# Two more buffers for the natural rows of q and k, a ring of 2560 tokens for x, and 512-token blocks in slots 48 to 143

## The chip, the core and the metric

The kernel runs on one core of a Trainium2 chip. The metric is the device time of one execution in microseconds (us). The core has five engines that run side by side and meet at semaphores: TensorE (PE) for matmuls, VectorE (DVE), ScalarE (ACT), GpSimd (POOL) and SyncE (SP). GpSimd, SyncE and ScalarE also issue DMAs, which 16 DMA engines carry out.

## The reference

Attention in a sliding window, and a two-layer network behind it, cut to what matters:

```python
q, k, v: (8, 8, 576, 64)                     # batch, heads, tokens, head width
scores = q @ k.T / sqrt(64)                  # only where |i - j| <= 32
attn   = softmax(scores) @ v
x      = attn.transpose(0, 2, 1, 3).reshape(8 * 576, 512)
h      = x @ w_in                            # (4608, 512) @ (512, 2048)
g      = h if h >= 1, 0 if h <= -1, else (h + 1)**2 / 4
out    = g @ w_out                           # (4608, 2048) @ (2048, 512)
```

## The kernel before, in words

The matmuls run in bf16. The kernel is one stream of **slots**, numbered by `a` in the loop at L497, with an order written out by hand. A slot does three things on TensorE:

- **the projection** `hp`: a piece of x @ w_in. In a narrow slot (L528 to L532) that is 256 columns of w_in for one block of 256 tokens: 8 matmuls of 256 columns (L491). In a wide slot (L510 to L518, slots `WIDE`, 56 to 135) it is 128 columns of w_in for two blocks together: 4 matmuls of 512 columns (L516). Eight narrow slots do one block, 16 wide slots do two. ACT and DVE make g from `hp` (L535 to L542) and write it to `gT`, which holds four blocks of 256 tokens; `home` says in which of the four a block lies. `hp` has two buffers in PSUM.
- **attention** of some later tokens, if the table `ev` has any for this slot (`run(a)` behind the projection, `run(a + 0.5)` at the slot's end).
- **the output**: matmuls of g @ w_out of earlier blocks (`pair` at L466 in the early slots, `unit` at L451 after that; from slot 40 on 3 units in a slot, from slot 72 on 4). ACT copies the sums out, SP stores them.

**Attention** of a batch of 576 tokens has five steps. `scores` or `scores8` does q @ k on TensorE, exp on ACT, and the mask on DVE. `sums` does attn @ v and the row sums on TensorE; its `end()` makes 1/sum with a Ln (L303) and an Exp (L304) on ACT; the product that gives x is put off (`muls`) and issued on DVE by `flush` (L309, L312), at the latest at the start of the next slot. Steps 0 and 1 are tokens 0 to 223 for the lower and the upper half of a group of heads (y1 = 0 and 1), steps 2 and 3 are tokens 224 to 479, step 4 is the rest for both. The list `sl` gives the slots: entry n has the `sums` of step 6 + n and the `scores` of step 7 + n, counted from batch 1 on.

**x** lies in `xT`, 512 rows of x as four groups of 128 partitions, in a ring of `RING` = 2304 tokens. The projection's matmuls go over the four groups in the order 0, 2, 1, 3: the first half of them reads y1 = 0, the second y1 = 1.

**q and k** of batches 2 to 7 come in natural rows (`load_nat`, L95 to L100, GpSimd's queue, f32 to bf16 on the way, 64 elements to a row) and are transposed by a DMA from the SP queue (`xpose`, L196 to L199) into `qT` (three buffers) and `kT` (three buffers). The natural rows have one buffer each for two tags, `n0` and `n1`: q of batch b has tag (b % 2), k the other. So q of batch b + 1 goes where k of batch b lies, and can't be loaded until that is transposed. v has three buffers (`load_v`). All these loads stand in one order on GpSimd, each behind the one before; a transpose stands on SP behind the stores of the slots before it. The loop issues the loads and the transposes of batches 3 to 7 in slots counted from the first scores of that batch (L419 to L425): loads 17 slots ahead, transposes 11 and 9.

The pool `early` (L120) holds what is used up to slot 1 only: the first rows of q and k and a helper for the mask. It stays allocated to the end.

Of the kernel before, what the change touches and what calls it, by code (L numbers as in the profile page):

```python
# [8 lines left out]
BF = mybir.dt.bfloat16  # L9
# [5 lines left out]
def kernel(  # L15
# [19 lines left out]
    nc = tc.nc  # L35
    B, H, S, D = q.shape
# [3 lines left out]
    NU = NY * S // 128  # L40
    MAIN = 480
    TAIL = S - MAIN
    RING = 4 * S
    PAD = 32
    WIDE = 56, 136
    LONG = 2

    const = ctx.enter_context(tc.tile_pool(name="const", bufs=1))
    nat = ctx.enter_context(tc.tile_pool(name="nat", bufs=2))
# [19 lines left out]
    w_out = const.tile([128, 16, DM], BF, name="w_out")  # L69
    xT = const.tile([128, NY, RING], BF, name="xT")  # L70
    gT = const.tile([128, 16, 4, 256], BF, name="gT")
# [3 lines left out]
    V, P, A = nc.vector, nc.gpsimd, nc.scalar  # L75


    qn, kn, vn = {}, {}, {}
    HD = (slice(0, 64), slice(64, 128))

    def load_half(half, t, h, eng=None, x=None):
# [12 lines left out]

    def load_nat(b, t):  # L95
        src, dst, nm = ((q, qn, "qn"), (k, kn, "kn"))[t]
        x = dst[b] = nat.tile([128, NU, 2, D], BF, name=nm, tag=f"n{(b + t) % 2}", bufs=1)
        for h in range(2):
            nc.gpsimd.dma_start(out=x[:, :, h], in_=src[b, NY * h:NY * h + NY].rearrange("y s d -> (y s) d")  # L99
                                .rearrange("(u p) d -> p u d", p=128))  # L100
# [16 lines left out]
        nc.gpsimd.dma_start(out=w_out[:, k0:k1, 256 * c:256 * c + 256],  # L117
                            in_=moe_w_out.rearrange("(ko ki) f -> ki ko f", ki=128)[:, k0:k1, 256 * c:256 * c + 256])

    early = ctx.enter_context(tc.tile_pool(name="early", bufs=1))  # L120
    q32 = early.tile([128, 2, S], FP, name="q32")
    for h in range(2):
        load_half(0, 0, h, (nc.sync, nc.scalar)[h], q32)
# [145 lines left out]
    def sums(b, y1, lo, hi, pool=ps_n):  # L269

        bb = two_banks(pool)
        w = hi - lo
        todo = []
        if lo < MAIN:
            ys, D0 = (y1,), w
            for par in range(2):
                a0 = max(lo, 32 * par)
                off = 32 - 64 * par
                todo.append((None, a0 - lo, hi - lo, lambda a, h, par=par, a0=a0, off=off: (
                    pt[b][HD[a], h, y1, par, a0 + off:hi + off])))  # L280
                for c2 in range(4):
                    q0, q1 = max(0, 128 * c2 - off, lo), min(128 * c2 + 128 - off, hi)
                    if q0 < q1:
                        todo.append((NC * y1 + 2 * c2 + par, q0 - lo, q1 - lo, lambda a, h, par=par, q0=q0, q1=q1, off=off: (
                            pt[b][HD[a], h, y1, par, q0 + off:q1 + off])))
        else:
            ys, D0 = (0, 1), 2 * w
            todo.append((None, 0, 2 * w, lambda a, h: pt8[b][HD[a], h].rearrange("p y j -> p (y j)")))
            for y in ys:
                todo.append((NC * y + 8, y * w, y * w + w, lambda a, h, y=y: pt8[b][HD[a], h, y]))  # L290
                for c in (None, NC * y + 7):
                    todo.append((c, y * w, y * w + 64, lambda a, h, y=y: pt[b][HD[a], h, y, 1, 448:512]))
        for n, (c, c0, c1, p) in enumerate(todo):
            o = D0 if c is None else 0
            for a in range(2):
                for h in range(2):
                    nc.tensor.matmul(bb[HD[h], a, o + c0:o + c1], ones[HD[a]] if c is None else vn[b][HD[a], c, h],  # L297
                                     p(a, h), start=n == 0, stop=True, skip_group_check=True)

        def end():  # L300
            lr = smp.tile([128, 2, 256], FP, name="lr", bufs=1)
            rc = smp.tile([128, 2, 256], FP, name="rc")
            A.activation(lr[:, :, :D0], bb[:, :, D0:2 * D0], AF.Ln)  # L303
            A.activation(rc[:, :, :D0], lr[:, :, :D0], AF.Exp, scale=-1.0)  # L304
            r0 = (b * S + lo) % RING
            o = xT.rearrange("p (a y) t -> p a y t", a=2)[:, :, ys[0]:ys[-1] + 1, r0:r0 + w]
            if len(ys) == 1:
                o = o[:, :, 0]
                muls.append(lambda: V.tensor_mul(o, bb[:, :, :D0], rc[:, :, :D0]))  # L309
            else:  # L310
                like = "p a (y j) -> p a y j"
                muls.append(lambda: V.tensor_mul(o, bb[:, :, :D0].rearrange(like, y=2), rc[:, :, :D0].rearrange(like, y=2)))  # L312
        return end
# [96 lines left out]
        at(a, seq[2 + n][0])  # L410
    for n, a in enumerate((18, 20, 26.5, 28)):
        at(a, seq[3 + n][1])
    sl = [30, 32, 35, 38, 41, 44, 47, 50, 52, 57, 60, 63, 66, 68, 72, 76, 79, 82, 86]
    sl += [90, 93, 96, 100, 104, 108, 111, 114, 118, 123]
    for n, a in enumerate(sl):
        at(a, seq[6 + n][0], seq[7 + n][1] if n < len(sl) - 1 else None)
    for t in range(2):
        at(10 + 1.5 * t, (tposes, 1, (t, 0), (t, 1)))
    loads, xps = {}, {16: [(2, 0)], 18: [(2, 1)]}  # L419
    for b in range(LONG + 1, B):  # L420
        a = sl[5 * (b - 1) - 7] - 17
        for t in range(3):
            loads.setdefault(a + t, []).append((b, t))
        for t in range(2):
            xps.setdefault(a + 6 + 2 * t, []).append((b, t))  # L425

    op = {}

    def home(t):

        return (3 - t % 4 if t % 4 in (0, 3) else t % 4) if WIDE[0] <= NF * t < WIDE[1] else t % 4

    def unit(x):

        tt, j = divmod(x, 16)
        if tt == NT // 128 - 1:
            half, n = divmod(j, 8)
            if n == 0:
                op[tt] = ps_o.tile([128, 256], FP, name="op", tag="op")
            cols = slice(256 * half, 256 * half + 256)  # L440
            for k in (2 * n, 2 * n + 1):
                nc.tensor.matmul(op[tt], gT[:, k, home(tt // 2), 128 * (tt % 2):128 * (tt % 2) + 128], w_out[:, k, cols],  # L442
                                 start=k == 0, stop=k == 15)
            if n == 7:
                osb = osp.tile([128, 256], FP, name="osb")
                A.copy(osb, op[tt])
                nc.sync.dma_start(out=out[128 * tt:128 * tt + 128, cols], in_=osb)
            return
        if j == 0:
            op[tt] = ps_o.tile([128, DM], FP, name="op", tag="op")  # L450
        nc.tensor.matmul(op[tt], gT[:, j, home(tt // 2), 128 * (tt % 2):128 * (tt % 2) + 128], w_out[:, j],  # L451
                         start=j == 0, stop=j == 15)
        if j == 15:
            osb = osp.tile([128, DM], FP, name="osb")
            A.copy(osb, op[tt])  # L455
            nc.sync.dma_start(out=out[128 * tt:128 * tt + 128, :], in_=osb)
# [40 lines left out]
    for a in range(NF * NB + 2 * NF):  # L497
# [11 lines left out]
        if a < NF * NB:  # L509
            if wide:  # L510
                n, f = divmod(a - WIDE[0], 2 * NF)
                t = WIDE[0] // NF + 2 * n
                r0 = TB * t % RING
                hp = ps_h.tile([128, 2, TB], FP, name="hp", tag="hp")
                for n, kk in enumerate((0, 2, 1, 3)):
                    nc.tensor.matmul(hp.rearrange("p n t -> p (n t)"), w_in[:, kk, 128 * f:128 * f + 128],  # L516
                                     xT[:, kk, r0:r0 + 2 * TB], start=n == 0, stop=n == 3)
                g = gT[:, f, home(t):home(t + 1) + 1:home(t + 1) - home(t)]  # L518
            else:
                t, f = divmod(a, NF)  # L520
                r0 = TB * t % RING
                if a in (0,):
                    hps = [ps_h.tile([128, 2, TB], FP, name="hp", tag="hp") for _ in range(2)]
                    for y in range(2):
                        for n in range(2):
                            project(hps[n], f + n, r0, [(j, y + 2 * m) for j in range(2) for m in range(2)], y == 0, y == 1)
                elif not hps:
                    pool, tag = (ps_o, "op") if a == 6 else (ps_h, "hp")  # L528
                    hps = [pool.tile([128, 2, TB], FP, name="hp", tag=tag)]
                    project(hps[0], f, r0, [(j, kk) for j in range(2) for kk in (0, 2, 1, 3)], True, True)  # L530
                hp = hps.pop(0)
                g = gT[:, 2 * f:2 * f + 2, home(t)]  # L532

            rr = ewp.tile([128, 2, TB], FP, name="rr")
            A.activation(rr, hp, AF.Relu, scale=0.5, bias=0.5)  # L535
            mx = ewp.tile([128, 2, TB], FP, name="mx")
            if a in two_on_act:
                A.activation(mx, rr, AF.Square)
                V.scalar_tensor_tensor(g, hp, 1.0, mx, op0=ALU.max, op1=ALU.min)
            else:  # L540
                V.tensor_max(mx, hp, rr)  # L541
                V.scalar_tensor_tensor(g, rr, 1.0, mx, op0=ALU.min, op1=ALU.mult)  # L542
# [8 lines left out]
        if a >= 40:  # L551
# [2 lines left out]
                unit(x)  # L554
            done += n
        run(a + 0.5)
        for x in xps.get(a, []):
            xpose(*x)

# [29 lines left out]
```

## Time and profile before

| | us |
|---|---|
| median of 3 runs | 309.26 (307.13 to 311.13) |
| the profiled execution, its own time | 308.08 |
| its span in the profile | 306.3 |
| DVE busy / ACT busy / POOL busy | 241.8 / 190.6 / 78.2 |
| projection, narrow (L491): 512 matmuls | 66.2 busy |
| projection, wide (L516): 320 matmuls | 82.1 busy |
| output (L451): 496 matmuls | 126.9 busy |
| DMA queue of GpSimd's loads | 103,136 packets, 18.06 MB |
| DMA queue of stores and transposes | 34,016 packets, 16.81 MB |

The busy time of a group is the time in which at least one of its instructions ran. [...] A line of waits says which engine and instruction waited, for what, for how many us in total, how often and how long at most. In a line of the timeline stand the start, the duration, the engine, the line of the kernel and the tiles that are written and read; a bracket at its end is the idle time of that engine before it and what ended it. TensorE's granted clock is full (1.00) in every stretch.

### The profile page before, as it was taken

The page shows a single profiled execution, that of the slowest core. Times are in us where ns is not written, and L with a number is a line of the kernel's source. Part 1 is how long each engine was busy: PE and PEld are TensorE (multiplying, and loading weights), DVE is VectorE, ACT ScalarE, POOL GpSimd, SP SyncE. Part 2 cuts the span into 40 slices and gives each one's busy share as a digit, 9 for nine tenths or more (in the row PEclk, how much of TensorE's full clock was granted, in tenths as well). Part 3 has the DMA queues.
Part 4 walks back from the last instruction along what each step waited for, and adds up shares of the span by engine and source line. Part 5 has one row for each costly group of instructions (what it writes and reads, how often), then busy time and mean ns, then how long its engine had stood idle before and what let it go on. Part 6 is the DMA issues. An engine that isn't in the chain of part 4 may idle for free.

```text
span 306.3 us, 7848 instructions
## 1 busy us (share of the span) xinstructions
PE 298.4 (97%) x3324; PEld 175.0 (57%) x3324; DVE 241.8 (79%) x378; ACT 190.6 (62%) x318; POOL 78.2 (26%) x94
## 2 busy tenths in 40 slices
PE   8889999999999999999999999999999999999995
PEld 3567878876666776544444444444445444446644
DVE  4278958879888999999988888888888888788700
ACT  3687796648757767667766766665667654444311
POOL 8896661037008204601800730000000000000000
PEclk9999999999999999999999999999999999999999
DMA  9999999989999996997999997551011000000121
GB/s 153 184 195 201 178 185 179 165 152 159 127 155 145 151 142 122 171 155 121 147 154 177 108 170 77 113 112 36 34 36 37 34 36 35 34 36 34 58 81 68
DMA packets 137331, 35.67 MB, mean 116 GB/s; under 512 B 122320, under 2 KB 133072, under 8 KB 137296
## 3 DMA queue, kind: packets, MB, share of 16 engines
q0 software_dynamic: 103136, 18.06, 80.2%
q1 hardware_dynamic: 34016, 16.81, 26.8%
q8 instruction: 26, 0.43, 0.6%
q10 hardware_dynamic: 144, 0.29, 0.4%
q14 instruction: 9, 0.07, 0.1%
HBM read 36.70 MB, written 9.44 MB: 151 GB/s over the span
## 4 chain that ended last, share of the span: by engine, by line
PE 85%; DMA 8%; POOL 3%; ACT 1%; issue 1%; DVE 0%; POOLq 0%; ACTq 0%
PE op L451 34%; PE hp L516 23%; PE hp L491 14%; DMA kT<-kn 7%; PE bb L297 5%; PE op L466 5%; PE bb L231 2%; DMA w_in<-in_moe_w_in_dram 2%; POOL w_in L112 1%; PE op L442 1%; POOL vn L107 1%; PE tp L191 1%; POOL kh L86 1%; POOL qh L86 0%; PE bb L210 0%
## 5 line engine op out<-in xcount | busy, mean ns | idle before, releaser
L535 ACT ACTIVATE rr<-hp 128x512 f32<-128x512 f32 x144 | 85.5, 595 | 84.5 <-PE hp L516 49.5
L451 PE MATMUL op<-w_out,gT 128*128 128x512 bf16 x496 | 126.9, 380 | 0.0
L541 DVE TENSOR_TENSOR mx<-hp,rr 128x512 f32<-128x512 f32 x139 | 95.8, 689 | 26.7 <-ACT rr L535 24.9
L542 DVE SCALAR_TENSOR_TENSOR gT<-rr,mx 128x512 bf16<-128x512 f32 x139 | 96.4, 694 | 4.8
L516 PE MATMUL hp<-xT,w_in 128*128 128x512 bf16 x320 | 82.1, 379 | 0.0
L451 PEld LDWEIGHTS <-gT 128*128 128x128 bf16 x496 | 46.1, 98 | 47.6
L491 PE MATMUL hp<-xT,w_in 128*128 128x256 bf16 x512 | 66.2, 273 | 1.7 <-DMA w_in<-in_moe_w_in_dram 1.5
L491 PEld LDWEIGHTS <-w_in 128*128 128x128 bf16 x512 | 49.2, 98 | 17.0 <-DMA w_in<-in_moe_w_in_dram 1.3
L516 PEld LDWEIGHTS <-w_in 128*128 128x128 bf16 x320 | 31.3, 98 | 37.8
L99 POOL DMA_DIRECT2D qn<-in_q_dram x12 | 14.6, 1222 | 92.2 <-DMA kT<-kn 90.1
L239 ACT ACTIVATE pt<-bb 128x1024 bf16<-128x1024 f32 (+1 forms) x33 | 32.9, 1002 | 6.1 <-PE bb L231 4.7
L107 POOL DMA_DIRECT2D vn<-in_v_dram x32 | 27.5, 893 | 5.1 <-DMA w_out<-in_moe_w_out_dram 2.9
L309 DVE TENSOR_TENSOR xT<-bb,rc 128x512 bf16<-128x512 f32 (+1 forms) x32 | 21.0, 657 | 9.8 <-ACT rc L304 8.9
L455 ACT COPY osb<-op 128x512 f32<-128x512 f32 x31 | 18.0, 581 | 12.4 <-PE op L451 12.1
L304 ACT ACTIVATE rc<-lr 128x512 f32<-128x512 f32 (+2 forms) x40 | 23.5, 587 | 1.3
L303 ACT ACTIVATE lr<-bb 128x512 f32<-128x512 f32 (+2 forms) x40 | 22.0, 550 | 0.2
L205 DVE TENSOR_TENSOR pt<-pt,mask 128x1024 bf16<-128x1024 bf16 (+1 forms) x33 | 20.3, 615 | 0.8 <-ACT pt L239 0.7
L297 PE MATMUL bb<-pt,ones 64*64 64x256 bf16 (+3 forms) x352 | 19.5, 255 | 0.2 <-DVE xT L309 0.2
L297 PE MATMUL bb<-pt,vn 64*64 64x128 bf16 (+3 forms) x712 | 18.3, 204 | 0.0
L297 PEld LDWEIGHTS <-ones 64*64 64x64 bf16 x352 | 10.2, 106 | 12.9 <-issue 12.8
L297 PEld LDWEIGHTS <-vn 64*64 64x64 bf16 x712 | 16.7, 107 | 0.1
L466 PE MATMUL op<-w_out,gT 128*128 128x256 bf16 x128 | 16.3, 273 | 0.0
(61 smaller groups left out, 139.2 us busy)
## 6 DMA issues: line engine op xcount, KB each, us to landing
out_dram<-osb SPq DMA_DIRECT2D x35, 256.0 KB, 2.7
vn<-in_v_dram POOLq DMA_DIRECT2D x32, 144.0 KB, 11.4
qn<-in_q_dram POOLq DMA_DIRECT2D x12, 288.0 KB, 7.0
kn<-in_k_dram POOLq DMA_DIRECT2D x12, 288.0 KB, 9.4
w_in<-in_moe_w_in_dram POOLq DMA_DIRECT2D x11, 128.0 KB, 5.0
w_out<-in_moe_w_out_dram POOLq DMA_DIRECT2D x4, 256.0 KB, 8.0
w_out<-in_moe_w_out_dram POOLq DMA_DIRECT2D x2, 512.0 KB, 12.4
kh<-in_k_dram POOLq DMA_DIRECT2D x4, 144.0 KB, 4.7
```

The source lines that it names most:

```text
L107: nc.gpsimd.dma_start(out=vn[b][64 * a:64 * a + 64, :, h], in_=v[b, y:y + 2].rearrange("y s d -> (y s) d") .rearrange("(c r) d -> r c d", ...
L239: A.activation(p, ps[:, :, :w * n].rearrange(like, y=m), AF.Exp, scale=D ** -0.5)
L297: nc.tensor.matmul(bb[HD[h], a, o + c0:o + c1], ones[HD[a]] if c is None else vn[b][HD[a], c, h], p(a, h), start=n == 0, stop=True, skip_g ...
L303: A.activation(lr[:, :, :D0], bb[:, :, D0:2 * D0], AF.Ln)
L304: A.activation(rc[:, :, :D0], lr[:, :, :D0], AF.Exp, scale=-1.0)
L451: nc.tensor.matmul(op[tt], gT[:, j, home(tt // 2), 128 * (tt % 2):128 * (tt % 2) + 128], w_out[:, j], start=j == 0, stop=j == 15)
L466: nc.tensor.matmul(o[:, tt], gT[:, j, p, 128 * tt:128 * tt + 128], w_out[:, j, 256 * half:256 * half + 256], start=not done, stop=len(done ...
L491: nc.tensor.matmul(hp[:, j], w_in[:, kk, 256 * f + 128 * j:256 * f + 128 * j + 128], xT[:, kk, r0:r0 + TB], start=first and n == 0, stop=l ...
L516: nc.tensor.matmul(hp.rearrange("p n t -> p (n t)"), w_in[:, kk, 128 * f:128 * f + 128], xT[:, kk, r0:r0 + 2 * TB], start=n == 0, stop=n == 3)
L535: A.activation(rr, hp, AF.Relu, scale=0.5, bias=0.5)
L541: V.tensor_max(mx, hp, rr)
L542: V.scalar_tensor_tensor(g, rr, 1.0, mx, op0=ALU.min, op1=ALU.mult)
```

## The change

- `WIDE` is 48 to 144. Wide blocks begin at even numbers, so a pair lies side by side in `gT`, and `home` goes.
- `RING` is 2560 tokens, ten blocks of 256, so that no pair of blocks goes over the ring's end. A product of `muls` that does go over it is issued in two parts.
- q and k have two buffers each. The second two are in a new pool, `nat2`, which is opened behind slot 1 in the room that the pool `early` gives back there. q and k of even batches go to `nat`, of odd batches to `nat2`.
- The list `sl` has other slots for 13 of its entries, 3 of them half slots (issued at the slot's end), and loads and transposes stand two slots later from the batch's first scores.

```diff
-    RING = 4 * S
+    RING = 4 * S + 256
-    WIDE = 56, 136
+    WIDE = 48, 144
+    nats = [nat]
...
-        x = dst[b] = nat.tile([128, NU, 2, D], BF, name=nm, tag=f"n{(b + t) % 2}", bufs=1)
+        x = dst[b] = nats[b % 2].tile([128, NU, 2, D], BF, name=nm, tag=f"n{t}", bufs=1)
...
-    early = ctx.enter_context(tc.tile_pool(name="early", bufs=1))
+    stack = ExitStack()
+    early = stack.enter_context(tc.tile_pool(name="early", bufs=1))
...
-            o = xT.rearrange("p (a y) t -> p a y t", a=2)[:, :, ys[0]:ys[-1] + 1, r0:r0 + w]
+            x = xT.rearrange("p (a y) t -> p a y t", a=2)[:, :, ys[0]:ys[-1] + 1]
             if len(ys) == 1:
-                o = o[:, :, 0]
-                muls.append(lambda: V.tensor_mul(o, bb[:, :, :D0], rc[:, :, :D0]))
+                n = min(w, RING - r0)
+                for c0, c1 in ((0, n), (n, w)):
+                    if c0 < c1:
+                        r = (r0 + c0) % RING
+                        muls.append(lambda c0=c0, c1=c1, r=r: V.tensor_mul(
+                            x[:, :, 0, r:r + c1 - c0], bb[:, :, c0:c1], rc[:, :, c0:c1]))
...
-    sl = [30, 32, 35, 38, 41, 44, 47, 50, 52, 57, 60, 63, 66, 68, 72, 76, 79, 82, 86]
-    sl += [90, 93, 96, 100, 104, 108, 111, 114, 118, 123]
+    sl = [30, 32.5, 35, 37, 39.5, 42, 44.5, 47, 51, 54, 57, 60, 63, 67, 72, 76, 79, 82, 86]
+    sl += [90, 93, 96, 100, 104, 108, 110, 114, 118, 123]
...
-        a = sl[5 * (b - 1) - 7] - 17
+        a = int(sl[5 * (b - 1) - 7]) - 15
...
-                g = gT[:, f, home(t):home(t + 1) + 1:home(t + 1) - home(t)]
+                g = gT[:, f, t % 4:t % 4 + 2]
...
+        if a == 1:
+            stack.close()
+            nats.append(ctx.enter_context(tc.tile_pool(name="nat2", bufs=1)))
```

The other places where `home` stood have `t % 4` or `tt // 2 % 4`.

## The prediction

> **What bounds the kernel now.** I read the page first, then the windows by stretch, the waits, and last the timeline of the places where the chain leaves TensorE. From the page (engines; busy tenths in 40 slices of 7.66 us):
>
> ```profile
> PE 298.4 (97%) x3324; PEld 175.0 (57%) x3324; DVE 241.8 (79%) x378; ACT 190.6 (62%) x318; POOL 78.2 (26%) x94
> ...
> PE   8889999999999999999999999999999999999995
> ...
> DMA  9999999989999996997999997551011000000121
> ```
>
> TensorE is busy 298.4 of 306.3 us. By windows, it is idle 3.6 us before 30 us, then 0.85 us in all up to 280 us. So after the start the time is TensorE's work plus any hole, microsecond for microsecond. The DMA row says the engines are nearly full up to slice 25 (190 us): the q, k, v loads and the transposes compete. The waits (us in total, times, longest):
>
> ```profile
> POOL qn L99 <- DMA kT<-kn: 90.1, 5, 19.3
> ...
> DVE xT L309 <- ACT rc L304: 8.9, 16, 4.1
> ...
> PE bb L231 <- DMA kT<-kn: 0.8, 2, 0.4
> ```
>
> The change aims at the first line: GpSimd idles 90.1 us because the load of the next batch needs the buffer that the running transpose still reads. What it costs TensorE is the last line only: 0.8 us, two holes of 0.41 us (at 92.3) and 0.44 us (at 118.7), the transposed keys of batches 3 and 4. The transposes as the SP queue issued them (start, us spent issuing):
>
> ```profile
> 50.27 6.64 SPq L198 DMA_TRANSPOSE qT<-qn  x1
> 57.01 6.76 SPq L198 DMA_TRANSPOSE kT<-kn  x1
> ...
> 74.92 7.65 SPq L198 DMA_TRANSPOSE qT<-qn  x1
> 82.74 5.99 SPq L198 DMA_TRANSPOSE kT<-kn  x1
> ```
>
> The first pair is batch 2: kT landed when GpSimd was released, 66.54, and TensorE's first scores of batch 2 start at 67.65. The slack is 1.1 us. The reader should see a wait of 90 us that costs 0.85, and a transpose that barely arrives.
>
> [...] From 84 to 86 us, transposes (q1) and loads (q0) side by side (packets, MB, share):
>
> ```profile
> q0 software_dynamic: 831, 0.11, 79.8%
> q1 hardware_dynamic: 828, 0.21, 79.8%
> ```
>
> That is 415 packets/us each. Alone, the transposes make 1,695 in the 2 us from 164 (847/us), the loads 2,411 from 103 (1,200/us). [...] The chain has four of 512 in 0.86 us and eight of 256 in 0.87 us[...].
>
> **The change, part by part.**
>
> *512-token blocks for 16 more slots (48 to 55, 136 to 143).* 8 matmuls of 256 become 4 of 512 in each: 16 x (0.87 - 0.86) = **-0.13 us** of the path at most. 64 weight loads fewer, hidden anyway (PEld 57%). ACT and DVE keep their instructions per slot. At the end, the last gT part of tokens 4096 on is now made in slot 143 and read 19 matmuls later: 19 x 0.216 = 4.1 us, against 2.3 us from the end of the last hp to its gT (288.0 to 290.3). Cover enough, 0; if the chain were 2 us late it would show as a hole at 292 us.
>
> *Ring of 2560 and the split.* Two DVE instructions more (32 columns split off 256, in batch 4): bounded by 2 x 0.69 us on DVE, which is 90% busy there, and not on TensorE's path; I take 0 (0 to 0.5).
>
> *When x must be ready.* The blocks now start at even 256s, so slot 48 needs tokens up to 2047 and slot 64 up to 2559. The new list puts the sums that finish them (upper half of the rows, y1 = 1) in slot 47 and slot 63: one slot ahead. Before, the nearest was two (118 for 120), and TensorE shows no hole there. The trace has the same sums with the same successor, in slot 66 (us, duration):
>
> ```profile
> 142.92 0.30 PE L297 MATMUL bb<-pt,ones 64*64 64x256 bf16 x4
> ...
> 144.09 0.59 ACT L303 ACTIVATE lr<-bb 128x512 f32<-128x512 f32 x1
> ...
> 144.24 1.03 PE L516 MATMUL hp<-xT,w_in 128*128 128x512 bf16 x4
> ...
> 144.72 0.63 ACT L304 ACTIVATE rc<-lr 128x512 f32<-128x512 f32 x1
> ...
> 145.46 0.68 DVE L309 TENSOR_TENSOR xT<-bb,rc 128x512 bf16<-128x512 f32 x1
> ```
>
> The next slot's projection starts at 144.24, and x is written at 146.14. The first two of its four matmuls read y1 = 0, which is ready; so TensorE can go to 144.24 + 0.43 = 144.67 and would then stand 146.14 - 144.67 = **1.5 us** at slot 48. (In the built program of the changed kernel the third matmul of slots 48, 64 and 112 has its own wait on DVE; 112 is two slots ahead, as 120 was.) At slot 64 only the first 32 columns count, so the wait ends after a short first part of the split: I take 0.15 us instead of 0.68, **+1.0 us**. Bounds: 0.7 to 2.2 and 0.4 to 1.6, for DVE's backlog either way (DVE 69.2 of 80 us in 40 to 120). Behind the waiting matmul stands everything else of TensorE; DVE and ACT wait for that, with nothing to do instead.
>
> *Four buffers for q and k.* GpSimd's order of loads is unchanged, only the waits are: the load of batch 3 waits for readers of the early tiles (slot 1, done by 20 us) and goes out at 47, after v of batch 2 (46.3), not at 66.5. That of batch 4 waits for the transposes of batch 2, and so on. The load queue is then hardly ever empty up to some 110 us (13.8 thousand packets a batch). What runs against it:
> - Batch 2. Up to 62.7 us the v load ran beside the transposes anyway (316 packets in the 2 us from 62). After that kT ran nearly alone: 62.7 to 66.4. Beside batch 3's loads its 2,304 packets take 2304/415 = 5.6 us, landing at 62.7 + 5.6 + 0.5 = 68.8 against 67.65: **+1.2 us** of hole in slot 26.5 (0 to 4).
> - Batch 3. Transposes no longer wait for their load (74.9); SP reaches them after the store of slot 27, at 72.5. Under load a pair measured 16.2 to 17.5 us (50.3 to 66.5, 101.2 to 118.7), the first 5.3 us with nothing moved; under load all the way I reckon 5.3 + 5.6 + 1.6 (the lull seen between the two, 61 to 62.6) + 5.6 = 18.1: landing 90.6. TensorE wants it in slot 37, one slot earlier than before, at 91.2. I take **+0.3** (0 to 5), and the old 0.41 goes.
> - Batch 4. Issue about 97.5, after the store of slot 39; landing 115.6, wanted in slot 51 at 119. 0, and the old 0.44 goes: **-0.85** for both.
> - Batches 5 to 7: issue follows the store before, landing has 6 us and more; the last two ran in 8.7 and less, and stay hidden.
>
> Loads and transposes stand two slots later in the program, which moves nothing by itself: GpSimd's loads follow buffers, SP's the stores ahead of them.
>
> Sum: -0.13 + 1.5 + 1.0 + 1.2 + 0.3 - 0.85 = **+3.0 us**. On the profiled execution (308.08, span 306.3 and 1.8 around it) that is 311.1; on the median of the three runs (309.26) 312.3. I take 311.7.
>
> **The rivals.**
> 1. As summed: 309.5 to 314.
> 2. The transposes lose nothing and DVE is early: -0.85 - 0.13 + 0.7 + 0.4 = +0.1, 308.2 to 309.4. For: 16 slots' worth of loads is taken out of the stretch after 66 us. Against: 1.1 us of slack and the even shares measured.
> 3. **Slower by over 2%.** The transposes of batches 2 and 3 are starved by the load queue. The 5.3 us in which they move nothing were measured with 7 to 9 thousand load packets outstanding; batch 3 may meet twice as many. Doubling it puts kT of batch 3 at 95.9, a hole of 4.7 us in slot 37, and batch 2 at its bound of 4: 3.0 + 4.4 + 2.8 = +10, 318. It decides once the two holes exceed 4.7 us together. [...]
> 4. Nothing new is late and the old holes go: -1.0, 307.1 to 308.3. Further down there is nothing: 0.85 us of holes is all there is after 30 us, so over 2% faster needs something the trace doesn't show.
> 5. The extra buffers don't free the loads (a reader of the early tiles comes late): the slot 48 and 64 waits alone, +2.4, 310.5.
>
> **How the numbers follow.** Chances: 0.47, 0.24, 0.22, 0.04, 0.03. 2% (6.2 us) is about what a measurement of this kernel can tell from no change; the runs before span 307.1 to 311.1. Over 2% slower is case 3 and a tail of case 1: 0.23. Over 2% faster: 0.03. The range 308 to 318 covers cases 1, 2 and the larger part of 3.
>
> **What would show it.** GpSimd's 90.1 us of waiting for kT shrinks and its load of batch 3 is issued near 47. The waits list has "PE hp <- DVE xT" twice, 1.5 and 1.0 us, in slots 48 and 64; "PE bb <- DMA kT" once, near 68 us. Wrong if TensorE has no hole near 68, if kT of batch 3 or 4 still ends a wait, or if holes stand in the stretch after 130 us.

## The result, and the profile after

| | before | after |
|---|---|---|
| median, us (6 runs each, one chip) | 309.24 (307.13 to 311.13) | 321.98 (318.74 to 323.9) |
| the profiled execution, its own time | 308.08 | 322.10 |
| its span | 306.3 | 320.3 |

The ratio, of the fast runs (five of the six of after), is 1.0406, with a 95% interval from 1.0335 to 1.0478. The change made the kernel 4% slower; the prediction had said 311.7 and at most 318.

From the page of the kernel after (the engines, then 40 slices of 8.0 us; PEclk is TensorE's granted clock, the share of its full clock that it was given, in tenths):

```profile
PE 297.0 (93%) x3222; PEld 169.7 (53%) x3260; DVE 242.6 (76%) x380; ACT 191.0 (60%) x318; POOL 78.2 (24%) x94
...
PE   8787999977996997999899999999999999999995
...
PEclk9999999997998999999999999999999999999999
DMA  9999999999999999999991651119000001000021
```

TensorE is busy for about as long as before (297.0 against 298.4 us; 38 of its matmuls are missing from the later trace, and matmuls at a lower clock count as busy for longer: four of 512 columns took 1.71 us at 0.50, from 102.70 to 104.41, and 0.86 at 1.00, from 66.80 to 67.66), but the span is 14.0 us longer. There are two holes, near 72 and 99 us, and at or behind each a slice whose digit for the clock is 7 or 8. The waits name what they wait for (us in total, times, longest):

```profile
POOL qn L100 <- DMA qT<-qn: 36.1, 3, 15.9
...
POOL vn L108 <- PE bb L233: 9.7, 2, 9.4
...
POOL kn L100 <- DMA kT<-kn: 7.4, 2, 4.8
...
PE bb L233 <- DMA kT<-kn: 5.6, 2, 3.4
```

GpSimd no longer stands 90 us for a buffer. TensorE stands 5.6 us for the transposed keys, where it stood 0.8. The timeline of TensorE has the places; the bracket is the idle time before the line:

```profile
73.35 0.42 PE L233 MATMUL bb<-qT,kT 64*64 64x128 bf16 x16 [3.37 <-DMA kT<-kn]
...
100.02 0.42 PE L233 MATMUL bb<-qT,kT 64*64 64x128 bf16 x16 [2.26 <-DMA kT<-kn]
...
110.70 1.03 PE L494 MATMUL hp<-xT,w_in 128*128 128x256 bf16 x8 [0.28 <-DVE mx L544]
...
120.64 1.03 PE L494 MATMUL hp<-xT,w_in 128*128 128x256 bf16 x8 [0.46 <-DVE mx L544]
...
124.89 0.59 PE L519 MATMUL hp<-xT,w_in 128*128 128x512 bf16 x2 [1.38 <-DVE xT L314]
...
154.24 0.59 PE L519 MATMUL hp<-xT,w_in 128*128 128x512 bf16 x2 [0.92 <-DVE xT L314]
```

The first two are the keys of batches 2 and 3, the last two x at slots 48 and 64. What comes after the first hole is seen in the windows of 1 us (stretch; busy time of PE, PEld, DVE, ACT, POOL; granted clock; DMA share; GB/s):

```profile
72.00:73.00 1.00, 0.00 (x0) 0.00 (x0) 0.00 (x0) 0.00 (x0) 0.00 (x0) 1.00 1.98 179
73.00:74.00 1.00, 0.65 (x19) 0.54 (x20) 0.00 (x0) 0.18 (x1) 0.00 (x0) 1.00 1.32 255
74.00:75.00 1.00, 1.00 (x7) 0.73 (x7) 0.12 (x1) 1.00 (x2) 0.00 (x0) 0.60 1.53 252
75.00:76.00 1.00, 0.78 (x3) 0.41 (x3) 0.76 (x2) 0.97 (x3) 0.43 (x1) 0.50 2.41 155
76.00:77.00 1.00, 1.00 (x5) 0.43 (x3) 0.99 (x2) 0.37 (x2) 0.79 (x1) 0.50 2.45 157
77.00:78.00 1.00, 1.00 (x8) 0.67 (x6) 0.69 (x1) 0.49 (x1) 0.69 (x1) 0.70 2.50 172
```

From 74 to 78 us TensorE is busy for 3.78 us at a clock of 0.50 to 0.70, and by the 1.71 against 0.86 us above a matmul takes twice as long at 0.50: 0.40 + 0.50 + 0.50 + 0.30 = 1.7 us lost. The second hole is followed by the same from 101 to 105 us (0.75, 0.50, 0.50, 0.54): 1.7 us again. So **a hole of 3.37 us cost 5.1, one of 2.26 cost 4.0**.

With both traces laid slot on slot (the start of ACT's first step on `hp` of each slot), the later kernel is behind by 2.2 us at slot 26, 7.4 at slot 34, 13.1 at slot 47, 14.1 at slot 72 and 14.0 at the end. Item by item:

| where the time went | us |
|---|---|
| start, up to slot 8: late weights | 2.16 |
| hole before the scores of batch 2, and its half clock | 3.37 + 1.70 |
| hole before the scores of batch 3, and its half clock | 2.26 + 1.71 |
| x at slots 48 and 64 | 1.38 + 0.92 |
| DVE late at two narrow slots (110.70, 120.64) | 0.28 + 0.46 |
| the two old holes, and the 16 wide slots (worked out) | -0.85 - 0.13 |
| sum | 13.3 of 14.0 |

The first item is not counted as the change's: up to slot 8 the two programs do the same work, and the delay there went from 0 to 4.2 us over the twelve profiles of this study. That it is chance is not shown: it was 0.1 us or less in all three profiles with before's pools and ring, and 0.1 to 4.2 in the nine others. But the single executions of before differ by more than 4 us too, and the whole change in its last form (e9 below) can't be told from before over 12 runs. The item limits what one profile or one ratio can tell, so the experiments are also read from slot 8 on, where after is behind by 11.9 us.

Why the keys are late is seen on the SP queue (start, us spent issuing):

```profile
51.95 7.01 SPq L200 DMA_TRANSPOSE qT<-qn  x1
59.06 8.12 SPq L200 DMA_TRANSPOSE kT<-kn  x1
...
78.17 7.40 SPq L200 DMA_TRANSPOSE qT<-qn  x1
85.73 7.69 SPq L200 DMA_TRANSPOSE kT<-kn  x1
```

From the issue of qT to the landing of kT, the pair of batch 2 took 21.4 us (51.95 to 73.35; before 16.3), that of batch 3 took 21.9 (78.17 to 100.02; before 17.4, 74.92 to 92.33). The two DMA queues in two stretches of batch 3's pair, 88.6 to 89.8 and 90 to 92 us (packets, MB, share):

```profile
q1 hardware_dynamic: 56, 0.01, 40.1%
q0 software_dynamic: 55, 0.01, 13.5%
```

```profile
q0 software_dynamic: 1768, 0.22, 174.8%
q1 hardware_dynamic: 366, 0.09, 34.4%
```

From 86 to 88 us the two queues moved equally many packets (817 and 818). Two things come on top. For 1.2 us, within the first transpose, hardly a packet starts in either queue (56 and 55); such a standstill of both queues also stands in the trace of before, from 61.4 to 62.4 us (17 and 44), and why it comes is open. And between the end of the first transpose and the start of the second the loads have the engines nearly to themselves (1,768 packets against 366). By the transposes' own packets (256 bytes each, 2,304 to a transpose), batch 3's pair took 5.5 us to its first packet, 14.3 from there to its last, and 2.1 from the last packet to the landing.

### The profile page after: what moved, and what is told of

Its sections match the earlier page's. It is cut to its first block, busy times and chain, and to the rows that moved or that the text cites. A ratio compares the mean times of both kernels' runs of the same rounds, so it can differ in the third digit from the quotient of the medians.

```text
span 320.3 us, 7686 instructions
## 1 busy us (share of the span) xinstructions
PE 297.0 (93%) x3222; PEld 169.7 (53%) x3260; DVE 242.6 (76%) x380; ACT 191.0 (60%) x318; POOL 78.2 (24%) x94
## 4 chain that ended last, share of the span: by engine, by line
PE 64%; DMA 19%; POOL 5%; DVE 3%; issue 2%; SPq 2%; ACT 2%; POOLq 0%; ACTq 0%
PE op L454 30%; PE hp L519 25%; DMA kT<-kn 9%; DMA kn<-in_k_dram 4%; DMA qn<-in_q_dram 4%; PE bb L299 4%; PE hp L494 3%; POOL w_in L113 2%; SPq L200 2%; DMA w_in<-in_moe_w_in_dram 2%; PE bb L233 2%; DVE mx L544 1%; PE op L445 1%; POOL vn L108 1%; ACT pt L241 1%
## 5 line engine op out<-in xcount | busy, mean ns | idle before, releaser
L454 PE MATMUL op<-w_out,gT 128*128 128x512 bf16 x462 | 121.3, 383 | 4.9 <-issue 4.5
L519 PE MATMUL hp<-xT,w_in 128*128 128x512 bf16 x382 | 98.6, 379 | 2.3 <-DVE xT L314 2.3
L519 PEld LDWEIGHTS <-w_in 128*128 128x128 bf16 x384 | 37.6, 98 | 48.0 <-issue 3.0
L494 PE MATMUL hp<-xT,w_in 128*128 128x256 bf16 x384 | 51.4, 279 | 3.6 <-DMA w_in<-in_moe_w_in_dram 2.4
L494 PEld LDWEIGHTS <-w_in 128*128 128x128 bf16 x384 | 37.2, 100 | 15.3 <-issue 4.6
L314 DVE TENSOR_TENSOR xT<-bb,rc 128x448 bf16<-128x448 f32 (+2 forms) x34 | 21.2, 627 | 10.4 <-ACT rc L306 9.7
L207 DVE TENSOR_TENSOR pt<-pt,mask 128x1024 bf16<-128x1024 bf16 (+1 forms) x33 | 20.3, 615 | 7.7 <-ACT pt L241 7.7
L458 ACT COPY osb<-op 128x512 f32<-128x512 f32 x31 | 18.1, 583 | 13.1 <-PE op L454 12.7
L233 PE MATMUL bb<-qT,kT 64*64 64x128 bf16 (+1 forms) x520 | 12.9, 217 | 5.9 <-DMA kT<-kn 5.6
L100 POOL DMA_DIRECT2D kn<-in_k_dram x12 | 14.5, 1212 | 11.5 <-DMA kT<-kn 7.4
## 6 DMA issues: line engine op xcount, KB each, us to landing
w_out<-in_moe_w_out_dram POOLq DMA_DIRECT2D x2, 512.0 KB, 11.7
```

Source lines behind the costliest of these rows:

```text
L454: nc.tensor.matmul(op[tt], gT[:, j, tt // 2 % 4, 128 * (tt % 2):128 * (tt % 2) + 128], w_out[:, j], start=j == 0, stop=j == 15)
L494: nc.tensor.matmul(hp[:, j], w_in[:, kk, 256 * f + 128 * j:256 * f + 128 * j + 128], xT[:, kk, r0:r0 + TB], start=first and n == 0, stop=l ...
```

## The experiments

Theory A: the second buffers let the loads out early, these delay the transposes, and the holes cost clock on top. Theory B: the rest of the change does it (list, ring, wide slots, x just in time). Ratios are to the kernel before.

### The change in two halves

e1_no_buffers is the kernel after with one buffer per tag again, e2_buffers_alone the kernel before with the second pool alone.

```diff
 e1, against after
-        x = dst[b] = nats[b % 2].tile([128, NU, 2, D], BF, name=nm, tag=f"n{t}", bufs=1)
+        x = dst[b] = nat.tile([128, NU, 2, D], BF, name=nm, tag=f"n{(b + t) % 2}", bufs=1)
...
-    stack = ExitStack()
+    stack = ctx
...
-        if a == 1:
-            stack.close()
-            nats.append(ctx.enter_context(tc.tile_pool(name="nat2", bufs=1)))
 e2: the same lines the other way round, in before
```

> The changed kernel with the two extra buffers undone (two buffers for q and k as before, early pool kept), all else as changed. Theory A (the early loads slow the transposes, and the holes of 3.37 and 2.26 us behind kT of batches 2 and 3 come from that, with the clock loss after them): GpSimd waits about 90 us for kT again, no hole behind kT is over 1 us, the clock stays 1.00, and what remains is the two waits for x at slots 48 and 64 (1.4 and 0.9 us): 1.003 to 1.010 of before. Theory B (the transposes are late because they stand two slots later, whatever the loads do): holes behind kT as in the changed kernel, 1.03 or more.

> The kernel before with the two extra buffers alone (wide slots, ring, slots of attention and transposes as before). Theory A: holes behind kT of batches 2 and 3 of about 3 and 2 us, each followed by a stretch at a lower clock, no wait of hp for x: 1.025 to 1.040 of before. Theory B: 0.995 to 1.005.

Without the buffers: 314.29 us, 1.0164 [1.0113, 1.0216]. The waits of its trace:

```profile
PE hp L519 <- DVE xT L314: 2.3, 2, 1.4
...
PE hp L494 <- DVE mx L544: 0.7, 2, 0.5
...
PE bb L233 <- DMA kT<-kn: 0.6, 1, 0.6
```

The large holes and their clock are gone, and x and DVE cost what they cost in after. From slot 8 on it is 3.3 us behind before, which would be 1.011. The ratio is above the range that A gave, 1.003 to 1.010: by the medians it is 5.0 us, and what the other 1.7 us are is open. Its profiled execution lost 4.2 us at the start, to late weights, and shows the clock fall too (the other three runs, at a mean clock of 1.000, took 313.39 to 314.35, and have no profile to say where):

```profile
28.21 3.22 PE L494 MATMUL hp<-xT,w_in 128*128 128x256 bf16 x16 [2.00 <-DMA w_in<-in_moe_w_in_dram]
```

```profile
27.00:28.00 1.00, 0.00 (x0) 0.00 (x0) 0.96 (x3) 0.57 (x2) 0.61 (x1) 0.76 1.44 197
...
29.00:30.00 1.00, 1.00 (x7) 0.72 (x5) 0.00 (x0) 0.00 (x0) 0.73 (x1) 0.50 1.38 198
```

The buffers alone: 314.5 us, 1.0193 [1.0132, 1.0254], 7.3 us behind from slot 8 on:

```profile
73.96 0.42 PE L233 MATMUL bb<-qT,kT 64*64 64x128 bf16 x16 [4.64 <-DMA kT<-kn]
...
101.78 0.42 PE L233 MATMUL bb<-qT,kT 64*64 64x128 bf16 x16 [1.85 <-DMA kT<-kn]
```

Half clock follows the first hole only (the page's digit for the clock is 7 from 70.9 to 78.8 us); after 1.85 us of idle it is 1.00 in each window of 1 us from 101 to 107. That is why it stays under the range that A gave, 1.025 to 1.040. The buffers account for about half or more (7.3 of 11.9 us by the profiles, 0.0193 of 0.0406 by the ratios). B alone is refuted, but both halves cost: 7.3 + 3.3 = 10.6 of 11.9. The two parts don't simply add up: in after the second hole is 2.26 us and costs its clock too, 0.4 and 1.7 more, but the first is 1.3 shorter than here; e1's own hole of 0.6 isn't there; and the two old holes (0.85), gone in both parts, were counted twice. That makes 11.7.

### Holding one load back, and moving the scores

e3_gate3 is after, with the loads of batch 3 held behind the transposed keys of batch 2 by a small copy on GpSimd. e4_scores_later moves the scores of batch 2 by one slot.

```diff
 e3
+    gate = const.tile([128, 1], BF, name="gate")
...
         for b, x in loads.get(a, []):
+            if (b, x) == (3, 0):
+                P.tensor_copy(gate, kT[2][:, 0:1])
 e4: the second of the two lists, for seq[3 + n][1]
-    for n, a in enumerate((18, 20, 26.5, 28)):
+    for n, a in enumerate((18, 20, 27.5, 29)):
```

> The changed kernel with one small GpSimd copy that reads a column of kT of batch 2 ahead of the loads of batch 3, so that these go out only when that transpose has landed, as before the change. Theory A: the first hole (3.37 us, and 1.9 us of lost clock) is gone, kT of batch 2 lands under 17 us after its qT was issued and not 21; the second hole stays, as batch 3's transposes still run beside loads, at 2 to 4 us: 1.020 to 1.030 of before. Theory B: both holes stay, 1.035 to 1.045.

> The changed kernel with the first two scores of batch 2 one slot later (27.5 and 29 for 26.5 and 28), loads unchanged. [...] the first hole falls to about 1.6 us, its stretch at 0.55 to 0.60 clock goes, and the time falls by 3 to 4 us against the changed kernel (1.028 to 1.032 of before). If the clock loss has another cause: 1.7 us less, and the low clock near 75 us stays.

e3: 319.26 us, 1.0325 [1.0265, 1.0385]. The pair of batch 2 took 15.6 us, and the first hole and its half clock are gone. But the pair of batch 3 still took 19.6 (75.47 to 95.08), and the second hole doubled, with a lower clock behind it (the page's digit is 7 from 94.6 to 102.5 us); A had given 2 to 4 us for it, and at most 1.030:

```profile
66.69 0.41 POOL L507 COPY gate<-kT 128x1 bf16<-128x1 bf16 x1 [19.07 <-DMA kT<-kn]
```

```profile
95.08 0.42 PE L234 MATMUL bb<-qT,kT 64*64 64x128 bf16 x16 [4.60 <-DMA kT<-kn]
```

So the load of batch 3 is the cause of the first hole. The second is not its sequel: TensorE, which is no longer late itself, comes to the keys of batch 3 earlier (90.48 us, against 97.76 in after). That it is the same collision one batch on is shown by e8 below.

e4: 317.1 us, 1.0234 [1.0163, 1.0306]. The first hole was halved, to 1.79 us, and a hole of 0.88 us followed in the slot's attention; the half clock stayed:

```profile
72.08 0.42 PE L233 MATMUL bb<-qT,kT 64*64 64x128 bf16 x16 [1.79 <-DMA kT<-kn]
...
74.35 0.40 PE L299 MATMUL bb<-pt,ones 64*64 64x224 bf16 x4 [0.88 <-DVE pt L207]
```

```profile
74.00:75.00 1.00, 0.65 (x23) 0.65 (x23) 0.97 (x3) 0.11 (x1) 0.00 (x0) 0.50 2.38 159
...
76.00:77.00 1.00, 1.00 (x4) 0.43 (x3) 0.45 (x1) 0.52 (x1) 0.36 (x1) 0.50 1.89 218
```

That the shorter hole would keep the clock was the author's estimate, which no run had shown. The clock fell all the same; most of what the edit gained is the second hole with its clock, which is gone here.

### Transposes without the loads of v

v of a batch is needed after its keys, but is loaded before them. e6_v_last (before) and e8_after_v_last (after) put v of batches 3 to 7 behind the transposed keys of the same batch.

```diff
-            loads.setdefault(a + t, []).append((b, t))
+            loads.setdefault(a + (0, 1, 9)[t], []).append((b, t))
...
+    gate = const.tile([128, 1], BF, name="gate")
...
             else:
+                P.tensor_copy(gate, kT[b][:, 0:1])
                 for n in range(4):
                     load_v(b, n)
```

> The kernel before with one change of order: v of batches 3 to 7 is loaded after kT of the same batch has landed (a small GpSimd copy that reads a column of kT ahead of it), so the transposes have the DMA engines to themselves. Theory A (a pair takes 17 us beside loads and 9 without): the pair of batch 3 takes 9 to 11 us instead of 17.4, kT of batches 3 and 4 lands 5 us or more ahead of its first scores, both holes of the kernel before (0.41 and 0.44 us) go: 0.994 to 1.001 of before. Rival (the length of a pair lies in the SP queue or in the transposes themselves): a pair stays at 16 us or more, and kT of batch 3 is no earlier.

> The changed kernel with v of batches 3 to 7 loaded after kT of the same batch. The loads of q and k of batch 3 still go out near 48 us, beside the transposes of batch 2. Theory A: the first hole (3 to 4.6 us, with a stretch at half clock) stays, as kT of batch 2 meets 9,216 load packets; the second goes, as batch 3's pair has the DMA engines to itself once q and k of batch 3 are in: 1.020 to 1.032 of before. Rival (the second hole comes from the two slots by which the transposes moved): it stays, 1.035 to 1.045.

e6: 308.24 us, 0.9981 [0.9955, 1.0007]. The pair of batch 3, with loads beside it at the start only (1,501 load packets from 78 to 80 us, 20 from 80 to 82, none from 82 to 84):

```profile
76.60 4.92 SPq L199 DMA_TRANSPOSE qT<-qn  x1
81.72 2.78 SPq L199 DMA_TRANSPOSE kT<-kn  x1
...
86.41 0.19 POOL L506 COPY gate<-kT 128x1 bf16<-128x1 bf16 x1 [13.33 <-DMA kT<-kn]
```

76.60 to 86.41 is 9.8 us, against 17.9 in before by the same mark, GpSimd's release. In time it buys nothing that can be told from no change.

e8: 318.44 us, 1.0312 [1.0204, 1.0421]. The pair of batch 3 took 9.2 us (79.73 to 88.92), and the second hole and its clock are gone. The first, of batch 2, which the edit doesn't touch, stays at 3.38 us with the half clock behind it (0.50 from 76 to 78 us).

### x one slot earlier

e5_x_earlier is e1, and e7_v_last_x_earlier is e1 with v last, both with the sums that finish x at the even 256s one slot ahead of where after has them.

```diff
-    sl = [30, 32.5, 35, 37, 39.5, 42, 44.5, 47, 51, 54, 57, 60, 63, 67, 72, 76, 79, 82, 86]
+    sl = [30, 32.5, 35, 37, 39.5, 41.5, 44, 46, 51, 54, 57, 59.5, 62, 67, 72, 76, 79, 82, 86]
```

> The changed kernel without the extra buffers (as in the first experiment), and with the sums that finish x for slots 48 and 64 one slot earlier (46 and 62 for 47 and 63; neighbours 41.5, 44 and 59.5 for 42, 44.5 and 60). If the two waits of hp for x are what the moved slots cost: both go (2.3 us), and of the two short waits of hp for DVE behind the half slots 39.5 and 44.5 (0.28 and 0.46 us) the second goes; nothing else is late: 2 to 3 us less than the first experiment, 1.003 to 1.010 of before. If the denser attention makes DVE the bound instead, waits of hp for DVE grow to the same sum: 1.012 to 1.018.

> Both of the above together on the wide slots 48 to 143 and the ring of 2560, two buffers. Theory A: no hole behind kT, none for x, at most 0.3 us for DVE: 0.994 to 1.003 of before, not to be told from the kernel before with v last, since 16 more wide slots are worth 0.13 us.

e5: 311.81 us, 1.0101 [1.0065, 1.0137]; e7: 309.51 us, 1.0028 [1.0002, 1.0053]. Both waits for x are gone in both. The small DVE waits stay, 0.28 and 0.53 us, the second now behind the new half slot 59.5. From slot 8 on they are 0.7 and 0.1 us behind before. For e7 that fits the ratio. For e5 it doesn't: 1.0101 is 3 us, and the one profile is of its fastest run. What the other runs lost is open. Since e7 differs from e5 only by v last, transposes that are late in some executions and not in others would fit, but no trace shows it.

### The buffers kept, the loads held

e9_four_buffers_held is the whole change, with e3's copy, v last, and x one slot earlier.

> The changed kernel with all four buffers, the loads of q and k of batch 3 held until kT of batch 2 has landed, v of every batch loaded after its kT, and the sums that finish x for slots 48 and 64 one slot earlier. Theory A (the buffers cost nothing; only what they let go out early does): as the same kernel with two buffers (1.003 measured), no hole behind kT, 0.998 to 1.008 of before. Rival (the place of the new buffers in memory or their waits cost time too): 1.015 or more.

309.0 us, 0.9997 [0.9959, 1.0035]. The transposes of batches 2 and 3 as SP issued them:

```profile
51.31 6.69 SPq L201 DMA_TRANSPOSE qT<-qn  x1
58.10 6.40 SPq L201 DMA_TRANSPOSE kT<-kn  x1
75.18 4.56 SPq L201 DMA_TRANSPOSE qT<-qn  x1
79.90 4.01 SPq L201 DMA_TRANSPOSE kT<-kn  x1
```

and what GpSimd waited for:

```profile
POOL gate L511 <- DMA kT<-kn: 102.5, 5, 34.6
...
POOL gate L507 <- DMA kT<-kn: 18.8, 1, 18.8
```

TensorE waits neither for the keys of batches 2 and 3 nor for x at slots 48 and 64. The same four buffers, the same ring and the same wide slots cost nothing that can be measured once GpSimd waits 121 us again: it was not the buffers, but what they let out early. There is no gain in them either.

### The kernel before, once more

> The kernel before once more, for its start: slots 0 to 8 came 0.1 to 4.2 us later in the five other profiles than in its first one, all with the same instructions there. If that is chance of the weights' arrival, its own second profile lies in that spread too and from slot 8 on has the spacing of the first within 0.5 us: 0.995 to 1.005.

309.4 us, 1.0026 [0.9993, 1.006]. Its start lies within 0.1 us of the first profile's, but it has no hole for the transposed keys at all and is 1.2 us shorter from slot 56 on, more than the 0.5 us that was expected at most. So the old holes of 0.41 and 0.44 us are marginal and come and go, and effects of about 1 us are below what single profiles tell here. None of the versions that were tried can be told to be faster than before.

## Why the prediction was wrong, step by step

- **TensorE bounds the kernel, and GpSimd's 90 us cost 0.85.** Right. In e9 GpSimd waits 121 us, and the time is that of before.
- **Wide slots, ring, split: 0.** Nothing of them is seen: e9 has all three at 0.9997 [0.9959, 1.0035]. The -0.13 is too small to be seen.
- **x at slots 48 and 64, +1.5 and +1.0.** Right: 1.38 and 0.92, and gone when the sums come a slot earlier (e5, e7, e9).
- **The loads go out early, that of batch 3 at 47.** Right in kind; it went at 50.74.
- **The transposes under load: the step that failed.** "Under load all the way I reckon 5.3 + 5.6 + 1.6 (the lull seen between the two, 61 to 62.6) + 5.6 = 18.1" was 21.9. The lag at the start (5.5) held, and so did the equal shares (817 and 818 packets in 2 us). The packets of both took 14.3 us instead of 5.6 + 1.6 + 5.6 = 12.8, and from the last packet to the landing it took 2.1, for which this sum has no term. The lull of 1.6 had been, for the most part, the standstill of both queues from 61.4 to 62.4 us; in after such a standstill came, and the stretch between the two transposes with it. So "+0.3" was 2.26: 3.8 us more for the pair, less 0.6 us of slack and 0.9 by which TensorE came later after the issue than reckoned. For batch 2 the same reckoning ("2304/415 = 5.6 us, landing at 62.7 + 5.6 + 0.5 = 68.8") gave "+1.2", and 3.37 was measured: the pair took 21.4 us where that makes 18.5. Its lag was 0.5 us longer, the packets of both took 1.2 more, the landing 1.1 more (1.6, not 0.5). The terms were taken from pairs that had the loads beside them for a part of the time only. Batch 4 had slack and made no hole, as predicted, though its pair took 20.3 us.
- **The clock, priced at nothing: the second error.** The sum has no term for it. No run had yet shown a clock under 1.00 behind a hole; that the holes reckoned here (0.3 to 1.5 us) cost none was the author's estimate. Holes of 2.00 and 2.26 us did cost it, one of 1.85 did not. What sorts the cases here is TensorE's busy time in a window of 3.413 us (last section): 1.65 and 1.32 us in the window ahead of the fall for the first two, 1.59 for the third, with no fall behind it. So, as an estimate from that, it also matters where in a window a hole falls. This was 3.4 of the 14.0 us.
- **Left out: DVE at the half slots.** 0.28 and 0.46 us behind the new half slots 39.5 and 44.5. There the put-off product for x stands at the head of DVE's next slot, ahead of what frees `hp`. The trace of after has it: DVE waits for `rc` (0.35 us), does the product from 109.42 on and only then `mx`, whose end releases TensorE at 110.70; the same from 119.30 to 120.64. e5, with another half slot, moved the second wait to it.
- **Rival 3**, with 0.22, named the mechanism and its threshold (the two holes over 4.7 us together; they are 5.63), but not the way: it doubled the lag at the start, which hardly grew, and it had no clock in its sum.
- **The start, 2.16 us of the profiled execution,** has no term in the prediction, and what sets it is open. Without it, the sum should have been near 11.9 instead of 3.0: 2.2 from the first hole, 2.0 from the second, 3.4 from the clock, 0.7 from DVE, which is 8.3 of the 8.9 missing.

## What to carry to other kernels

A wait for a buffer may be what keeps a bulk load off the DMA engines while a transfer that somebody needs is under way: before adding the buffer, lay the transfers it sets free over the ones on the critical path, and add up the latter at their price with the load beside them throughout (here 21.4 and 21.9 us for a pair in after, 9.2 and 9.8 with v held back). If the buffer is wanted, hold the load by a wait on what must land first. And price a hole in TensorE with the clock behind it (1.7 us behind each of the two of after), not by its length alone. By the figures of the next section, and as an estimate from them, a hole of 2.0 us can cost it (if it lies in one window: 3.4 - 1.4), and one of 4.0 would wherever it falls.

## What the runs showed of the hardware that was not expected

- TensorE's granted clock changed at multiples of 3.413 us. In the twelve traces every stretch at 0.50 that the trace's end doesn't cut off lasts 3.413 us, and the stretches at 1.00 between two of them are whole multiples of it (in after 23.893 and 215.04 us, 7 and 63 windows). The clock fell behind holes of 2.26, 3.37, 3.38, 4.60 and 4.64 us, within one of 2.00, and within the second of two close together (1.79 and 0.88); not behind single ones of 1.85, 1.46 and 1.38. It fell 0.7 us before work resumed (e1) to 1.5 us after (the second hole of after). The length of the hole doesn't sort these, but TensorE's busy time in the window before does. Of the 1,072 windows of 3.413 us into which this divides the twelve traces, the 17 in which TensorE was busy (as the profile models it) for 1.40 us or less were all followed by half clock, 11 of them at the kernel's end, the 1,052 with 1.72 or more never; of three between, one was (1.65) and two were not (1.45, 1.59). First the second hole of after, then the two holes of e4, last the second hole of e2, each time the window that has most of the idle time and the next one (columns as above):

```profile
98.09:101.50 3.41, 1.32 (x22) 0.89 (x24) 1.30 (x2) 1.01 (x2) 0.84 (x1) 1.00 1.83 233
101.50:104.91 3.41, 3.41 (x15) 1.76 (x13) 2.55 (x4) 1.52 (x4) 3.24 (x4) 0.50 2.40 159
```

```profile
70.51:73.92 3.41, 1.40 (x24) 1.06 (x25) 1.28 (x3) 1.78 (x3) 1.23 (x1) 1.00 1.70 227
73.92:77.33 3.41, 2.65 (x30) 1.64 (x31) 2.29 (x4) 1.31 (x3) 1.21 (x1) 0.50 2.12 200
```

```profile
98.33:101.74 3.41, 1.59 (x38) 1.08 (x36) 2.77 (x4) 0.68 (x2) 0.00 (x0) 1.00 1.81 140
101.74:105.15 3.41, 3.22 (x35) 2.21 (x37) 1.60 (x3) 2.63 (x5) 2.67 (x3) 1.00 2.10 200
```

- A pair of transposes took 9.2 us (batch 3 in e8) and 9.8 (in e6) with v held back. It took 16.3 and 17.4 us in before, with 8,023 load packets from 50 to 67 us and 7,264 from 75 to 92, and 21.4, 21.9 and 20.3 in after, with 12,882 from 52 to 73, 14,084 from 78 to 100 and 10,273 from 108 to 128. SP's issue of one took 2.6 to 3.3 us in the last two pairs of before (39 load packets from 161 to 169 us, none from 193 to 206) and 6.0 to 7.7 in the four ahead of them, 7.0 to 8.1 in the first three of after. So a long issue was a sign here that other packets were in the way.
